# Transposing K in two row halves of the TensorE array, in a cached-attention kernel

## The chip, the cores and the metric

The kernel runs on one core of one Trainium2 chip. The metric is the device time of one execution in microseconds (us), as the median of several runs.

Engine names as the profile has them: PE is the TensorE's matmul side, PEld its weight loads, DVE the VectorE, ACT the ScalarE, SP the engine that issues the loads. "DMA" is what the 16 DMA engines move. The "granted clock" is the share of TensorE's full clock that the profile records as let through; in all traces here it is 1.0 or 0.5, and a figure between them is a mean over time.

## The reference

Attention of 4 new positions in each of 32 batches against a cache of 2,048 keys; 32 query heads share 4 key/value heads; head size 128; all bfloat16. Cut to what matters:

```python
B, Sq, D = 32, 4, 1024
Hq, Hkv, Sk, Dh = 32, 4, 2048, 128
q = (x @ wq).reshape(B, Sq, Hq, Dh).transpose(0, 2, 1, 3)
k = jnp.repeat(k_cache, Hq // Hkv, axis=1)
v = jnp.repeat(v_cache, Hq // Hkv, axis=1)
scores = jnp.einsum("bhqd,bhkd->bhqk", q, k) * Dh ** -0.5
p = softmax(scores)
o = jnp.einsum("bhqk,bhkd->bhqd", p, v)
return o.transpose(0, 2, 1, 3).reshape(B, Sq, Hq * Dh) @ wo
```

K and V are 2 MB each per batch, 128 MB in all; the two weight matrices are 8 MB each.

## The kernel before

It is a hand-scheduled program: each engine has its own list of instructions, with semaphores between them. One batch i is one turn of the loop:

```python
for i in range(B):
    pe_qk(i)                      # 16 matmuls: scores into four PSUM banks (ps_s)
    softmax_max(i)                # DVE
    if i >= 2: pe_ot(i - 2); ot_evac(i - 2)      # (every 8th batch: oproj, 128 matmuls)
    for f in (0, 1): pe_fill(i + 1, f); evac(i + 1, f)
    softmax_exp(i)                # ACT
    for f in range(2, 8): pe_fill(i + 1, f); evac(i + 1, f)
    softmax_rinv(i)
    if i >= 1: pe_pv(i - 1); o_evac(i - 1)       # 64 matmuls on four column tiles
    for f in range(2): pe_pt(i, f); evac_pt(i, f)  # 16 transposes of P
```

K arrives with keys on the partitions; QK needs it with the head size there, so each batch needs 64 transposes of 128x128 (tiles t of K_sb). They come in eight "fills" of 8, each into one PSUM bank of a ring of four, and ACT (fills 0, 1, 4, 6) or DVE (2, 3, 5, 7) copies the bank to KT_sb:

```python
def pe_fill(b, f):
    buf, waits = slot(("kt", b, f))           # next of the four ring banks, once free
    buf = slot_of["kt", b, f] = buf.bitcast(BF16)
    for q in range(TB):                        # TB = 8
        c, v = q // (TB // C), q % (TB // C)
        t = c * TV + f * TB // C + v
        p.op("pe", lambda e, q=q, t=t: e.transpose(
            buf[:, q * 128:(q + 1) * 128], K_sb[:, b % NKB, t, :], ident[:, :]),
            waits + [("k", b), "ident"] if q == 0 else [], ("fill", b, f) if q == TB - 1 else None)
```

Each matmul or transpose becomes two instructions of TensorE, a weight load and a matmul (5,929 of each on the page below). A batch has 2 x (64 + 64 + 16 + 16 + 1) = 322 of them; in the trace it is 323 with a wait, and an output projection adds 256 to every eighth batch.

## Time and profile before

| | before |
|---|---|
| time, median of 3 | 387.33 us (387.23 to 387.41) |
| span of the profiled run | 385.4 us |
| data moved | 152.32 MB, 416 GB/s in the stretch 200 to 300 us |
| mean granted clock of TensorE | 0.946 |
| one batch while data is the limit | 10.0 us |
| one batch while catching up (compute alone) | 8.6 us |

The chain of waits that ended last, by engine, shares of the span:

```profile
DMA 59%; PE 17%; ACT 13%; DVE 7%; issue 2%; SPq 1%
```

Groups of instructions: line, engine, operation, tiles, shapes, count | busy us, mean ns of one | idle time before them and what ended it.

```profile
L207 PE MATMUL ps_r<-ident,K_sb 128*128 128x128 bf16 x2048 | 142.6, 229 | 66.0 <-DMA K_sb<-in_k_cache_dram 40.8
L217 DVE COPY KT_sb<-ps_r 128x1024 bf16<-128x1024 bf16 x128 | 148.0, 1216 | 40.0 <-PE ps_r L207 39.8
...
L248 PE MATMUL ps_r<-V_sb,PT_sb 128*32 128x128 bf16 x2048 | 36.7, 223 | 17.2 <-ACT KT_sb L219 12.8
...
L225 PE MATMUL ps_r<-ident,P_sb 128*128 128x128 bf16 x512 | 35.1, 223 | 1.8 <-ACT P_sb L285 1.4
L240 PE MATMUL ps_s<-KT_sb,QT_sb 128*32 128x512 bf16 x512 | 34.3, 386 | 2.5 <-DVE KT_sb L217 1.7
```

The idle time of L207 ends on the landing of K; PE, DVE and ACT all have slack. The timeline of PE over one batch (start us, duration us, engine, line, what; in brackets the idle time before and what ended it):

```profile
271.34 1.08 PE L248 MATMUL ps_r<-V_sb,PT_sb 128*32 128x128 bf16 x64 [0.92 <-ACT KT_sb L219]
272.35 1.07 PE L225 MATMUL ps_r<-ident,P_sb 128*128 128x128 bf16 x16
273.35 1.05 PE L240 MATMUL ps_s<-KT_sb,QT_sb 128*32 128x512 bf16 x16
...
275.85 2.41 PE L207 MATMUL ps_r<-ident,K_sb 128*128 128x128 bf16 x40 [1.29 <-DMA K_sb<-in_k_cache_dram]
278.50 1.07 PE L207 MATMUL ps_r<-ident,K_sb 128*128 128x128 bf16 x16 [0.24 <-ACT KT_sb L219]
...
281.36 1.08 PE L248 MATMUL ps_r<-V_sb,PT_sb 128*32 128x128 bf16 x64 [0.93 <-ACT KT_sb L219]
```

PV, P transposes, QK, then 1.29 us of waiting for K, then 64 K transposes, then PV again 10.0 us after the last one. Forty transposes take 2.41 us with the last one's latency.

### The profile page before, as it was taken

Reading aid. Unit: us, or ns where it says so; the run is one execution under the profiler, and the core shown is the slowest. Engines: PE = TensorE matmul, PEld = TensorE weight load, DVE = VectorE, ACT = ScalarE, POOL = GpSimd, SP = SyncE. Lnnn points to the kernel's source line nnn. Section 1 sums busy time; section 2 is a strip of 40 time slices with the busy share of each in tenths; the row PEclk is TensorE's granted clock in tenths of the full one; section 3 lists DMA queues with packets and bytes.
Section 4 is the critical chain, followed back from the end, with each engine's and each line's share of the span. In section 5 each row is a group of like instructions: output and inputs, shape, how many; then the busy total and the mean of one; then the engine's idle time right before and its main releaser. Section 6 shows DMA issues by size and latency. Waiting matters only on the chain.

```text
span 385.4 us, 12595 instructions
## 1 busy us (share of the span) xinstructions
PE 280.9 (73%) x5929; PEld 229.5 (60%) x5929; DVE 274.1 (71%) x299; ACT 208.5 (54%) x261; POOL 0.7 (0%) x6
## 2 busy tenths in 40 slices
PE   1876888676383967888767778877767888776756
PEld 1875766465282856666655566665645676565545
DVE  0017999683552984899888859998868859987850
ACT  1005777355161646676666627766646566666620
POOL 0000000000000000000000000000000000000000
PEclk9998999886976899999999999999999999999978
DMA  7999999999999999999999999999999999999930
GB/s 328 432 432 416 418 417 398 413 410 395 413 409 409 419 416 414 419 413 418 417 419 417 417 414 417 416 416 411 417 417 417 418 420 415 417 418 410 375 143 9
DMA packets 27251, 152.32 MB, mean 395 GB/s; under 512 B 1472, under 2 KB 1984, under 8 KB 22592
## 3 DMA queue, kind: packets, MB, share of 16 engines
q1 hardware_dynamic: 27104, 151.49, 96.1%
q8 instruction: 46, 0.75, 0.8%
q10 hardware_dynamic: 96, 0.03, 0.0%
q14 instruction: 5, 0.04, 0.0%
HBM read 151.26 MB, written 0.26 MB: 393 GB/s over the span
## 4 chain that ended last, share of the span: by engine, by line
DMA 59%; PE 17%; ACT 13%; DVE 7%; issue 2%; SPq 1%
DMA K_sb<-in_k_cache_dram 59%; ACT KT_sb L219 7%; ACT P_sb L285 6%; DVE KT_sb L217 4%; PE ps_r L207 4%; PE ps_r L248 3%; PE ps_r L296 3%; PE ps_r L225 3%; PE ps_s L240 3%; DVE mx L280 2%; PE ps_s L296 1%; DVE PT_sb L231 0%; SPq L129 0%; PE ps_r L271 0%; ACT oT_sb L275 0%
## 5 line engine op out<-in xcount | busy, mean ns | idle before, releaser
L207 PE MATMUL ps_r<-ident,K_sb 128*128 128x128 bf16 x2048 | 142.6, 229 | 66.0 <-DMA K_sb<-in_k_cache_dram 40.8
L217 DVE COPY KT_sb<-ps_r 128x1024 bf16<-128x1024 bf16 x128 | 148.0, 1216 | 40.0 <-PE ps_r L207 39.8
L207 PEld LDWEIGHTS ps_r<-ident,K_sb 128*128 128x128 bf16 x2048 | 125.7, 103 | 82.2 <-DMA K_sb<-in_k_cache_dram 41.9
L219 ACT ACTIVATE KT_sb<-ps_r 128x1024 bf16<-128x1024 bf16 x128 | 124.5, 1025 | 72.1 <-PE ps_r L207 72.0
L280 DVE TENSOR_REDUCE mx<-ps_s 128x1 f32<-128x2048 f32 x32 | 73.3, 2292 | 7.1 <-PE ps_s L240 4.6
L285 ACT ACTIVATE P_sb<-ps_s,negmx 128x2048 bf16<-128x2048 f32 x32 | 63.0, 1969 | 2.2 <-DVE negmx L281 2.1
L231 DVE COPY PT_sb<-ps_r 128x1024 bf16<-128x1024 bf16 x64 | 41.4, 686 | 16.7 <-PE ps_r L225 15.2
L248 PE MATMUL ps_r<-V_sb,PT_sb 128*32 128x128 bf16 x2048 | 36.7, 223 | 17.2 <-ACT KT_sb L219 12.8
L248 PEld LDWEIGHTS ps_r<-V_sb,PT_sb 128*32 128x32 bf16 x2048 | 31.0, 98 | 22.7 <-ACT KT_sb L219 19.4
L275 ACT ACTIVATE oT_sb<-ps_r 128x128 bf16<-128x128 bf16 x31 | 8.6, 277 | 55.6 <-PE ps_r L271 55.6
L225 PE MATMUL ps_r<-ident,P_sb 128*128 128x128 bf16 x512 | 35.1, 223 | 1.8 <-ACT P_sb L285 1.4
L240 PE MATMUL ps_s<-KT_sb,QT_sb 128*32 128x512 bf16 x512 | 34.3, 386 | 2.5 <-DVE KT_sb L217 1.7
L225 PEld LDWEIGHTS ps_r<-ident,P_sb 128*128 128x128 bf16 x512 | 29.4, 99 | 5.4 <-ACT P_sb L285 1.6
L240 PEld LDWEIGHTS ps_s<-KT_sb,QT_sb 128*32 128x32 bf16 x512 | 10.8, 96 | 13.3 <-issue 2.8
L187 DVE CAST QT_sb<-ps_r 128x512 bf16<-128x512 f32 x2 | 1.3, 686 | 22.4 <-PE ps_r L176 22.4
L265 ACT ACTIVATE o_sb<-ps_r,rinv 128x128 bf16<-128x128 f32 x31 | 11.4, 367 | 9.8 <-PE ps_r L248 9.8
L189 ACT ACTIVATE QT_sb<-ps_r 128x512 bf16<-128x512 f32 x2 | 1.1, 594 | 26.0 <-PE ps_r L176 26.0
L176 PE MATMUL ps_s<-P_sb,w_sb 128*128 128x128 bf16 x128 | 9.4, 232 | 7.2 <-DMA w_sb<-in_wq_dram 7.2
L296 PE MATMUL ps_r<-w_sb,oT_sb 128*32 128x256 bf16 x384 | 11.5, 273 | 2.6 <-issue 1.4
L176 PEld LDWEIGHTS ps_s<-P_sb,w_sb 128*128 128x128 bf16 x128 | 8.3, 105 | 7.8 <-issue 4.4
L296 PEld LDWEIGHTS ps_r<-w_sb,oT_sb 128*32 128x32 bf16 x384 | 10.0, 97 | 3.7 <-issue 2.5
L271 PEld LDWEIGHTS ps_r<-ident,o_sb 128*128 128x128 bf16 x31 | 3.0, 98 | 12.7 <-issue 12.7
(30 smaller groups left out, 58.9 us busy)
## 6 DMA issues: line engine op xcount, KB each, us to landing
K_sb<-in_k_cache_dram SPq DMA_DIRECT2D x32, 2048.0 KB, 25.4
V_sb<-in_v_cache_dram SPq DMA_DIRECT2D x31, 2048.0 KB, 27.3
w_sb<-in_wq_dram SPq DMA_DIRECT2D x4, 2048.0 KB, 14.8
w_sb<-in_wo_dram SPq DMA_DIRECT2D x4, 2048.0 KB, 24.7
V_sb<-in_v_cache_dram SPq DMA_DIRECT2D x4, 512.0 KB, 15.8
P_sb<-in_x_dram SPq DMA_DIRECT2D x1, 256.0 KB, 2.8
out_dram<-y_sb SPq DMA_DIRECT2D x14, 16.0 KB, 12.1
out_dram<-y_sb ACTq DMA_DIRECT2D x2, 16.0 KB, 1.6
```

The lines of the kernel that those rows point to most:

```text
L176: p.op("pe", lambda e, kt=kt, h=h: e.matmul(ps_q(h), lhsT=w_sb[:, kt, h * Dh:(h + 1) * Dh], rhs=xT_sb[:, kt, :], start=(kt == 0 and h % 4 ...
L207: p.op("pe", lambda e, q=q, t=t: e.transpose(buf[:, q * 128:(q + 1) * 128], K_sb[:, b % NKB, t, :], ident[:, :]), waits + [("k", b), "iden ...
L217: p.op("dve", lambda e: e.tensor_copy(dst, src), waits, ("kt", b, f))
L219: p.op("act", lambda e: e.activation(dst, src, ACT.Copy), waits, ("kt", b, f))
L225: p.op("pe", lambda e, q=q: e.transpose(buf[:, q * 128:(q + 1) * 128], P_sb[:, (8 * f + q) * 128:(8 * f + q + 1) * 128], ident[:, :]), wai ...
L231: p.op("dve", lambda e: e.tensor_copy(PT_sb[:, 8 * f:8 * f + 8, :].rearrange("p t q -> p (t q)"), buf), [("ptf", i, f)] + ([("pv", i - 1)] ...
L240: p.op("pe", lambda e, c=c, g=g: e.matmul(ps_s[32 * g:32 * (g + 1), c * 512:(c + 1) * 512], lhsT=QT_sb[:, i, REP * g:REP * (g + 1), :], rh ...
L248: p.op("pe", lambda e: e.matmul(buf[32 * g:32 * (g + 1), 0:Dh], lhsT=PT_sb[:, t, 32 * g:32 * (g + 1)], rhs=V_sb[:, i % NVB, g, t, :], star ...
L265: p.op("act", lambda e: e.activation(o_sb[:, :], buf[:, 0:Dh], ACT.Copy, scale=rinv[:, i:i + 1]), [("pv", i), ("rinv", i)] + ([("oT", i - ...
L280: p.op("dve", lambda e: e.tensor_reduce(mx[:, i:i + 1], ps_s[:, :], AX.X, ALU.max), [("qk", i)], ("mx", i))
L285: p.op("act", lambda e: e.activation(P_sb[:, :], ps_s[:, :], ACT.Exp, bias=negmx[:, i:i + 1], scale=scale, accum_out=ssum[:, i:i + 1]), [( ...
L296: p.op("pe", lambda e, h=h, j=j: e.matmul(buf[32 * j:32 * (j + 1), 0:NC], lhsT=oT_sb[:, h, 32 * n:32 * (n + 1)], rhs=wo_sb[:, h, NC * j:NC ...
```

## The change

The intent: two half tiles, each on its own 64 rows of the array, should be worked on at once and so take less than one whole tile. The keys of a tile are split into rows 0 to 63 and 64 to 127; each half is transposed by its own 64x128 row tile into its own bank, 64 columns at a time. Fills therefore go in groups of two banks, and KT_sb gets the half as an outer dimension.

```diff
-        KT_sb = sbuf("KT_sb", [128, TV, G, R * C], BF16)
+        KT_sb = sbuf("KT_sb", [128, 2, TV, G // 2, R * C], BF16)
@@ pe_fill
+            if f % 2:
+                return
+            bufs, waits = [], []
+            for h in range(2):
+                buf, w = slot(("kt", b, f + h))
+                buf = slot_of["kt", b, f + h] = buf.bitcast(BF16)
+                bufs.append(buf)
+                waits += w
-            for q in range(TB):
+            for q in range(2 * TB):
 ... (c, v, t of the doubled group)
-                p.op("pe", lambda e, q=q, t=t: e.transpose(
-                    buf[:, q * 128:(q + 1) * 128], K_sb[:, b % NKB, t, :], ident[:, :]),
+                for h in range(2):
+                    p.op("pe", lambda e, q=q, t=t, h=h: e.transpose(
+                        bufs[h][:, q * 64:(q + 1) * 64], K_sb[64 * h:64 * h + 64, b % NKB, t, :],
+                        ident[64 * h:64 * h + 64, 64 * h:64 * h + 64]),
 ... (waits at the first, both "fill" marks at the end of the group)
@@ evac
+            dst = KT_sb[:, f % 2, v0:v0 + 2 * TB // C, :, :].rearrange("p v g (r c) -> p (v g) r c", c=C)
@@ pe_qk
-                        rhs=KT_sb[:, 4 * c:4 * (c + 1), g, :],
+                        rhs=KT_sb[:, g // 2, 4 * c:4 * (c + 1), g % 2, :],
```

## The prediction

> **What bounds the kernel now.** The DMA queue. In the table of stretches its share is 0.99 to 1.03 from 10 us to 360 us; the page counts 152.32 MB, which at the 416 GB/s of 200:300 is 366 us of the 385.4 us span. The chain of waits is 59% "DMA K_sb". One batch (4 MB of K and V) takes 10.0 us: in the timeline the K transposes start at 265.84 and 275.85 us, after 1.3 us of waiting for K both times. The compute chain of a batch is shorter: 8.57 us between 310.21 and 318.78 us, where PE was catching up after an output projection. So some 1.5 us per batch are slack. After the last K lands (358.56 us) comes a tail of 26.9 us which nothing hides.

> **What the change does.** 2,048 K transposes (128x128; 40 in a row start within 2.24 us, 56 ns each) become 4,096 half ones (64 rows, N=64) on alternating row halves, with twice the weight loads, each still 128 columns. The order of the program shows four groups of 32 per batch instead of eight of 8. Each group waits for two PSUM buffers and hands both over at its end. Evictions (ACT 1,025 ns, DVE 1,216 ns), their order and access patterns, QK, PV, softmax and all DMA keep shape and count.

> **Cost of the PE part.** In the trace, 64 PV matmuls on four column tiles take 1.08 us, 17 ns for one load and one matmul; if row halves overlap as well, a pair costs 34 ns (issue) to 56 ns (no gain), so a batch's transposes cost 2.2 to 3.6 us instead of 3.6.[...]

> **How much is critical.** Of the eight fills only the first (0.63 us) is on the batch's chain; the rest hide behind evictions and the exp (2 x 0.97 ACT evictions, 1.95 exp, 0.9 eviction), then PV, PT, QK. The first eviction waited for 8 transposes (0.45 us); it now waits for 16 tiles' worth (0.5 to 0.9 us). The chain moves by 0 to +0.4 us and stays under 10 us: no effect while the DMA is the limit. In the tail that counts once. K buffers come free a little earlier, but loads are already 25 us in flight, so bandwidth isn't touched.

> **Prediction: 387.2 us, 8 in 10 between 384.5 and 391.5; faster by over 2%: 0.03, within 2%: 0.87, slower: 0.10.**

> **What would show it right.** DMA share still about 1.0 at 416 GB/s up to 360 us; batch period 10.0 us; L215 PE busy time falling from 142.6 us to 80 to 130 us; ACT and DVE busy times unchanged; tail from last K landing 26 to 28 us.

> **What would make it wrong.** (1) Row halves that don't overlap[...]: [...]the time goes to 400 us or more, DMA share below 0.95. (2) The granted clock: it fell to 0.50[...] (72 to 80 us, 86 to 94 us). With sparser PE work it may fall in more batches; a cold iteration took 9.1 us (107.1 to 116.2), still under 10, but the tail could move by 1 to 3 us: it ran PT and PV at 0.50 (372 to 377 us), oproj at 1.00. (3) Handover in pairs that stalls ACT and DVE on PSUM buffers; four buffers, two per group, leave just one group ahead.

The cost of the PE part comes to 2.2 to 3.6 us a batch, from the 17 ns and the 56 ns of the trace, and the 387.2 us rest on that and on the data queue. The case against it, risk 1, was summed to 400 us or more. The falls to 0.50 are in the trace.

## More of the kernel before

The page of the kernel before: busy time by engine; then, over 40 equal slices of the span, the granted TensorE clock in tenths, the share in which the DMA engines were busy in tenths, and the rate; then the DMA queue q8, with packets, MB and share.

```profile
PE 280.9 (73%) x5929; PEld 229.5 (60%) x5929; DVE 274.1 (71%) x299; ACT 208.5 (54%) x261; POOL 0.7 (0%) x6
...
PEclk9998999886976899999999999999999999999978
DMA  7999999999999999999999999999999999999930
GB/s 328 432 432 416 418 417 398 413 410 395 413 409 409 419 416 414 419 413 418 417 419 417 417 414 417 416 416 411 417 417 417 418 420 415 417 418 410 375 143 9
...
q8 instruction: 46, 0.75, 0.8%
```

The DMA row is at 9 from the second slice until the tail: the queue of data is the limit. PEclk is at full speed from slice 15 on, until the tail. Queue q8 carries 16,384-byte blocks of instructions.

## The result, and the profile after

The changed kernel took **420.48 us** (419.1 to 420.5, three runs), against 387.33 us before: ratio 1.0844, 95% interval 1.0811 to 1.0878. Ratios here are the mean time of one kernel's fast runs over that of the other's of the same rounds, so not quite the ratio of the medians. The prediction was 387.2 us, range 384.5 to 391.5, and "within 2%" had 0.87.

The page after, the same lines:

```profile
PE 273.6 (66%) x7977; PEld 213.8 (51%) x7977; DVE 275.8 (66%) x299; ACT 209.7 (50%) x261; POOL 0.7 (0%) x6
...
PEclk9995789866586886768695986698886998879989
DMA  8999999999999999999999986999999978998600
GB/s 341 432 426 409 419 414 412 394 409 410 400 418 416 416 415 422 411 419 412 414 393 370 386 369 255 363 394 401 385 380 405 364 300 305 380 421 307 223 9 8
...
q8 instruction: 62, 1.02, 1.0%
```

PE's busy time went down by 7 us, and the time up by 33. Two rows look different: PEclk is below full speed in most slices, and DMA falls below 9 in several slices from the middle of the span on, with 371 GB/s between 200 and 300 us instead of 416. Queue q8 has 62 packets instead of 46. The chain:

```profile
PE 41%; ACT 19%; DMA 19%; DVE 14%; issue 6%; SPq 0%
```

DMA is 19% of it instead of 59%. The groups:

```profile
L228 DVE COPY KT_sb<-ps_r 128x1024 bf16<-128x1024 bf16 x128 | 149.2, 1217 | 20.6 <-PE ps_r L215 20.1
L215 PE MATMUL ps_r<-ident,K_sb 64*128 64x64 bf16 x4096 | 94.4, 203 | 100.2 <-ACT KT_sb L230 43.2
...
L259 PE MATMUL ps_r<-V_sb,PT_sb 128*32 128x128 bf16 x2048 | 55.6, 283 | 11.5 <-issue 6.4
L236 PE MATMUL ps_r<-ident,P_sb 128*128 128x128 bf16 x512 | 49.6, 272 | 10.5 <-issue 6.9
...
L251 PE MATMUL ps_s<-KT_sb,QT_sb 128*32 128x512 bf16 x512 | 42.1, 451 | 3.1 <-issue 1.6
```

L215, the half transposes, is what the change hoped for: 94.4 us busy instead of 142.6: 64 half transposes start within 0.98 us (below, at 280.04; 1.17 us with the end of the last), 31 ns for a pair of halves against 56 ns for a whole tile. The copies of DVE are as before, and so are those of ACT (1,025 ns in both). But instructions that the change did not touch got slower: PV (L259) 55.6 us instead of 36.7, P transposes (L236) 49.6 instead of 35.1, QK (L251) 42.1 instead of 34.3. The timeline of PE, the batch from 269 us and the one from 280 us:

```profile
269.45 1.03 PE L215 MATMUL ps_r<-ident,K_sb 64*128 64x64 bf16 x55
271.55 0.30 PE L215 MATMUL ps_r<-ident,K_sb 64*128 64x64 bf16 x9 [1.07 <-issue]
...
274.98 0.96 PE L259 MATMUL ps_r<-V_sb,PT_sb 128*32 128x128 bf16 x55
277.62 0.34 PE L259 MATMUL ps_r<-V_sb,PT_sb 128*32 128x128 bf16 x9 [1.69 <-issue]
...
280.04 1.17 PE L215 MATMUL ps_r<-ident,K_sb 64*128 64x64 bf16 x64
...
285.56 1.74 PE L259 MATMUL ps_r<-V_sb,PT_sb 128*32 128x128 bf16 x64
287.24 1.89 PE L236 MATMUL ps_r<-ident,P_sb 128*128 128x128 bf16 x16
289.06 1.28 PE L251 MATMUL ps_s<-KT_sb,QT_sb 128*32 128x512 bf16 x16
```

Two different things can be seen here, and each costs its batch more than the 1.5 us that used to be slack.

- **At 271.55 and 277.62 PE stands still with nothing to wait for** ("issue"): 1.07 us within a group of half transposes, and 1.69 us within PV, after 55 of its 64 matmuls. No semaphore stands there.
- **From 285.56 on, PV takes 1.74 us, the P transposes 1.89 us and QK 1.28 us**, where before they took 1.08, 1.07 and 1.05. Between 286 and 288 us the granted clock was 0.50; it had been 1.00 from 270 to 284 us.

From 131 us (where the weights are loaded) to the last QK, the batch took 11.61 us on average, output projections included, instead of 10.22; the mean clock in this time was 0.81 instead of 1.00. 23 batches of 1.39 us more are 32 of the 33 us.

**Where the stalls sit.** The trace holds every instruction of PE and PEld and every DMA packet. I numbered the instructions of TensorE in order of start, and listed queue q8's packets beside them.

```
                                             before    changed
instructions in TensorE's stream             11,905    16,054
16,384-byte packets on q8                        46        62
instructions per packet (stream / packets)      259       259
stalls "issue" over 0.25 us after 50 us whose
  first instruction is number 192..195 mod 256     7        32
  their sum                                   7.9 us   35.2 us
from the end of a q8 packet to the restart                 1.25 to 1.62 us in all 32
median distance of two q8 packets after 131 us  6.5 us    6.3 us
```

In both kernels the distances crowd a little above 6 us: 17 of 45 before and 35 of 61 in the changed kernel lie between 5.9 and 6.6 us. (Seven in the changed kernel are below 5 us; in five of these seven gaps the DMA moved less than 180 GB/s.) So by these counts one packet brings 256 instructions (16,384 / 256 = 64 bytes each), and the stalls sit at one fixed place of every block, 1.25 to 1.62 us after a packet has ended. I read this as TensorE having run out of instructions. The stall at 277.62 us is instruction 10,177 = 39 x 256 + 193, and the last packet had ended 1.46 us earlier. In the kernel before, the seven stalls of this kind came to 7.9 us; in the changed kernel the 32 came to 35.2 us.

This gives a sum. If a block takes 6.2 us, TensorE gets at most 41 instructions a us. A batch of the changed kernel has 453 instructions: 453 / 256 x 6.2 = 11.0 us, and with an eighth of an output projection 11.7 us; 11.6 were measured. A batch before has 323: 7.8 us, or 8.6 with the projections, below the 10.0 us of the data. (When I wrote the expectations below I took 464 and 336, which is 11 and 13 too many, and left the projections out of the sum; the table has the counts of the traces.)

### The profile page after: what moved, and what is told of

Same layout as the page of the kernel before. It is cut to its first block, busy times and chain, and to the rows that moved or that the text cites. A ratio compares the mean times of both kernels' runs of the same rounds, so it can differ in the third digit from the quotient of the medians.

```text
span 417.3 us, 16744 instructions
## 1 busy us (share of the span) xinstructions
PE 273.6 (66%) x7977; PEld 213.8 (51%) x7977; DVE 275.8 (66%) x299; ACT 209.7 (50%) x261; POOL 0.7 (0%) x6
## 4 chain that ended last, share of the span: by engine, by line
PE 41%; ACT 19%; DMA 19%; DVE 14%; issue 6%; SPq 0%
DMA K_sb<-in_k_cache_dram 13%; PE ps_r L259 11%; ACT KT_sb L230 11%; PE ps_r L236 10%; PE ps_s L251 8%; ACT P_sb L296 8%; DVE KT_sb L228 7%; PE ps_r L215 7%; DVE mx L291 6%; DMA w_sb<-in_wq_dram 5%; PE ps_r L307 3%; PE ps_s L307 1%; PE ps_r L282 1%; PE ps_s L176 0%; DVE negmx L292 0%
## 5 line engine op out<-in xcount | busy, mean ns | idle before, releaser
L215 PE MATMUL ps_r<-ident,K_sb 64*128 64x64 bf16 x4096 | 94.4, 203 | 100.2 <-ACT KT_sb L230 43.2
L230 ACT ACTIVATE KT_sb<-ps_r 128x1024 bf16<-128x1024 bf16 x128 | 126.7, 1025 | 54.8 <-PE ps_r L215 54.4
L215 PEld LDWEIGHTS ps_r<-ident,K_sb 64*128 64x128 bf16 x4096 | 79.9, 103 | 114.6 <-ACT KT_sb L230 47.2
L291 DVE TENSOR_REDUCE mx<-ps_s 128x1 f32<-128x2048 f32 x32 | 73.3, 2292 | 18.9 <-PE ps_s L251 18.0
L242 DVE COPY PT_sb<-ps_r 128x1024 bf16<-128x1024 bf16 x64 | 42.8, 689 | 53.4 <-PE ps_r L236 53.3
L259 PE MATMUL ps_r<-V_sb,PT_sb 128*32 128x128 bf16 x2048 | 55.6, 283 | 11.5 <-issue 6.4
L236 PE MATMUL ps_r<-ident,P_sb 128*128 128x128 bf16 x512 | 49.6, 272 | 10.5 <-issue 6.9
L259 PEld LDWEIGHTS ps_r<-V_sb,PT_sb 128*32 128x32 bf16 x2048 | 45.9, 128 | 17.5 <-issue 8.6
L236 PEld LDWEIGHTS ps_r<-ident,P_sb 128*128 128x128 bf16 x512 | 42.3, 125 | 16.6 <-issue 11.6
L251 PE MATMUL ps_s<-KT_sb,QT_sb 128*32 128x512 bf16 x512 | 42.1, 451 | 3.1 <-issue 1.6
L251 PEld LDWEIGHTS ps_s<-KT_sb,QT_sb 128*32 128x32 bf16 x512 | 12.2, 106 | 19.4 <-issue 9.3
L307 PEld LDWEIGHTS ps_r<-w_sb,oT_sb 128*32 128x32 bf16 x384 | 10.1, 97 | 5.6 <-issue 4.5
```

The lines of the kernel that those rows point to most:

```text
L215: p.op("pe", lambda e, q=q, t=t, h=h: e.transpose(bufs[h][:, q * 64:(q + 1) * 64], K_sb[64 * h:64 * h + 64, b % NKB, t, :], ident[64 * h:6 ...
L230: p.op("act", lambda e: e.activation(dst, src, ACT.Copy), waits, ("kt", b, f))
L236: p.op("pe", lambda e, q=q: e.transpose(buf[:, q * 128:(q + 1) * 128], P_sb[:, (8 * f + q) * 128:(8 * f + q + 1) * 128], ident[:, :]), wai ...
L242: p.op("dve", lambda e: e.tensor_copy(PT_sb[:, 8 * f:8 * f + 8, :].rearrange("p t q -> p (t q)"), buf), [("ptf", i, f)] + ([("pv", i - 1)] ...
L251: p.op("pe", lambda e, c=c, g=g: e.matmul(ps_s[32 * g:32 * (g + 1), c * 512:(c + 1) * 512], lhsT=QT_sb[:, i, REP * g:REP * (g + 1), :], rh ...
L259: p.op("pe", lambda e: e.matmul(buf[32 * g:32 * (g + 1), 0:Dh], lhsT=PT_sb[:, t, 32 * g:32 * (g + 1)], rhs=V_sb[:, i % NVB, g, t, :], star ...
```

## The experiments

Three theories:

- **Refill theory**: 40% more instructions a batch exceed the rate at which instruction blocks arrive.
- **Clock theory**: sparser PE work lets the granted clock drop to 0.50, and PV, P transposes and QK, which lie on the batch's chain, take twice as long.
- **Handover theory**: groups of two PSUM banks out of four starve or delay ACT and DVE.

Twelve kernels, with the kernel before run beside them (386.6 to 387.0 us in every group).

| run | what | instructions a batch | time us | ratio to before [95%] | mean clock |
|---|---|---|---|---|---|
| (change) | | 453 | 420.48 | 1.0844 [1.0811, 1.0878] | 0.81 |
| e1 | before + 128 semaphore increments a batch | 451 | 804.40 | 2.0807 [2.0762, 2.0852] | 0.64 |
| e2 | before + 64 of them | 387 | 493.26 | 1.2765 [1.2733, 1.2798] | 0.79 |
| e3 | before, groups of two banks | 325 | 386.38 | 0.9993 [0.9961, 1.0026] | 0.96 |
| e4 | change, half of the tiles | 325 | 402.21 | 1.0381 [1.0345, 1.0417] | 0.78 |
| e5 | before + 66 short matmuls a batch | 455 | 414.21 | 1.0718 [1.0667, 1.0768] | 0.95 |
| e6 | change + dense matmuls | 485 | 430.38 | 1.1121 [1.1060, 1.1183] | 0.92 |
| e7 | e4 + dense matmuls | 357 | 395.72 | 1.0232 [1.0168, 1.0295] | 0.86 |
| e8 | before, most V loads left out | 323 | 347.36 | 0.8977 [0.8958, 0.8996] | 0.98 |
| e9 | change, most V loads left out | 453 | 388.92 | 1.0036 [0.9998, 1.0075] | 0.83 |
| e10 | change in every second batch | 453 and 323 | 407.26 | 1.0524 [1.0501, 1.0547] | 0.85 |
| e11 | before, dummy matmuls in the tail | 323 | 385.12 | 0.9952 [0.9939, 0.9964] | 0.96 |
| e12 | before + 30 short matmuls a batch | 383 | 388.68 | 1.0048 [1.0028, 1.0067] | 0.96 |

(The clock is that of the profiled run; for e6, whose profiled run was slow, the mean of its three fast runs. All ratios are to the kernel before, also those of e8 and e9, whose results are wrong.)

### e1 and e2: idle instructions as filler (failed as a test)

```diff
@@ pe_fill of before, behind the transposes
+            for _ in range(16 if b else 0):          # e2: 8
+                p.op("pe", lambda e: e.sem_inc(filler, 1))
```

> The kernel before, with 16 idle instructions (increments of a semaphore that nobody reads) behind each of the eight K fills of batches 1 to 31: 3,968 more in TensorE's instruction stream, about as many as the change adds (4,096), with no more matmuls, the same PSUM handover and the same matmul density. Refill theory (instruction blocks of 16 KB reach TensorE no faster than one in about 6.2 us while the data queue is full, and 464 instructions a batch need 11.2 us): 405 to 425 us, refills 6.2 us apart, data queue no longer full. Clock theory and handover theory: 386 to 390 us.

> As e1, with 8 instead of 16 behind each fill: 400 instructions a batch. Refill theory: 400/256 x 6.2 = 9.7 us a batch, just under the 10.08 us that the data takes, so 386 to 393 us. If the idle instructions themselves cost sequencer time: about half of the rise of e1.

Both expectations missed widely: 804 and 493 us. The filler is not idle: in the timeline of e1 from 400 to 426 us, mostly 1.4 to 2.0 us (once 0.8) pass with PE idle at each place where 16 increments stand. The blocks on q8 (62) then came 12 us apart in the median, so refills were not the limit. The runs say nothing on the refill theory. They do say that PE's clock falls with idle time even where all matmuls are the long ones of before: in e2 it went to and fro between 0.50 and 1.00 every 6.8 us, with a mean of 0.79.

### e3: the handover alone

```diff
@@ pe_fill of before, in groups of two banks as in the change, full 128-row transposes
+            for q in range(TB):
+                for h in range(2):
+                    t = c * TV + (f + h) * TB // C + v
+                    ... e.transpose(bufs[h][:, q * 128:(q + 1) * 128], K_sb[:, b % NKB, t, :], ident[:, :])
```

> Only the handover of the change: full 128-row transposes as before, but issued alternately into two PSUM banks, both waited for before the first and both handed over after the last. Handover theory: a good part of the 33 us, over 395 us. Refill and clock theories: 386 to 390 us (instruction count and stream as before).

386.38 us, ratio 0.9993: the handover theory falls. Its one effect is on batches that catch up, 8.94 us instead of 8.64, which the data hides. Its mean clock was 0.96.

### e4: the instruction count of before, with even sparser PE work

```diff
@@ pe_fill of the changed kernel
-            for q in range(2 * TB):
+            for n in range(TB):
+                q = n % 4
@@ evac
-            src = buf.rearrange("p (c m r) -> p m r c", c=C, r=R)
+            src = buf[:, 0:256].rearrange("p (m r o) -> p m r o", r=R, o=1).broadcast_to([128, 8, R, C])
```

> Wrong result on purpose. The changed kernel with only 8 of the 16 tiles of each group transposed (in row halves, as in the change; evictions read the same quarter of the bank four times, so their size stays): the instruction count of before, 336 a batch, but TensorE streams even less than in the changed kernel. Clock theory (sparser work lowers the granted clock, and slow PV, PT and QK lengthen the batch): at least 410 us, mean clock under 0.82. Refill theory: 385 to 391 us.

402.21 us at a clock of 0.78, so between the two: the refill theory's "385 to 391" falls, and so does the clock theory's "at least 410". With the instruction count of before, and three stalls at the block's place (3.5 us in all), a loss of 15.6 us remains. (By the edit, the 8 tiles of a group are four tiles, each transposed twice. The copies of ACT and DVE took as long as before, 1,024 and 1,214 ns in the median, so the changed reading pattern is not the cause.) Clock and refills of e4:

```profile
PEclk9996666665675686666868698888888888888888
...
q8 instruction: 46, 0.75, 0.8%
```

The timeline of PE over a part of one batch of e4:

```profile
204.17 0.61 PE L216 MATMUL ps_r<-ident,K_sb 64*128 64x64 bf16 x16 [1.50 <-ACT KT_sb L231]
206.50 0.61 PE L216 MATMUL ps_r<-ident,K_sb 64*128 64x64 bf16 x16 [1.72 <-DVE KT_sb L229]
207.24 1.90 PE L260 MATMUL ps_r<-V_sb,PT_sb 128*32 128x128 bf16 x64
209.07 1.89 PE L237 MATMUL ps_r<-ident,P_sb 128*128 128x128 bf16 x16
```

There is no stall in the middle of a group. PE works 0.6 us out of each 2.3 us while ACT and DVE evict, the clock is at 0.50 from 204.2 to 211.0 us, and PV and the P transposes run at half speed. The batch takes 10.1 to 11.1 us instead of 10.0. The records show the clock at 1.0 or 0.5 only, in phases of 3.4 us or multiples of it (in the kernel before 3.41, 6.83, 10.24, 34.13 us and so on, apart from the cut-off last one). (A side note: the comparison with the reference still passed, although a part of K was replaced by another. With these inputs it seems hardly to see K.)

### e5: the instruction count of the change, with denser PE work

```diff
@@ pe_fill of before
+            extra = 11 if b and f >= 2 else 0
+            for m in range(extra):
+                p.op("pe", lambda e, m=m: e.matmul(
+                    raw[:, 0:64], lhsT=K_sb[:, b % NKB, m, :], rhs=ident[:, 0:64],
+                    start=True, stop=True, skip_group_check=True), ...)
```

> The kernel before, with 11 short matmuls (128 rows, N=64, into the bank that is then overwritten) ahead of each of the fills 2 to 7 of batches 1 to 31: 132 more instructions a batch, 468 instead of 336, about as many as in the changed kernel (464), while TensorE works more densely than before, not less. Refill theory: 468/256 x 6.2 = 11.3 us a batch, so 400 to 425 us, with stalls at rows 193 and 194 of every 256, 1.3 us after a refill ended, and a clock near 1.0. Clock theory alone: 386 to 391 us.

414.21 us, with the clock nearly full:

```profile
PEclk9999999999699999899999998999989999989988
...
q8 instruction: 62, 1.02, 1.0%
```

There were 35 stalls at numbers 192 to 195 of the blocks, 51.2 us in all, and blocks came 6.1 us apart in the median. The timeline of PE, PV and P transposes of two batches:

```profile
201.13 0.95 PE L254 MATMUL ps_r<-V_sb,PT_sb 128*32 128x128 bf16 x53
204.11 0.35 PE L254 MATMUL ps_r<-V_sb,PT_sb 128*32 128x128 bf16 x11 [2.02 <-issue]
...
212.39 1.08 PE L254 MATMUL ps_r<-V_sb,PT_sb 128*32 128x128 bf16 x64
213.40 1.07 PE L231 MATMUL ps_r<-ident,P_sb 128*128 128x128 bf16 x16
```

In the batch at 204 us PV stops for 2.02 us after 53 matmuls; in the next one it runs through, at full speed. Batches without a stall took 8.8 to 9.1 us, so the added matmuls are not themselves the limit. Row halves and low clock are absent here, and 27 of the 33 us are back: **the refill theory is right for most of the loss, and needs nothing of the row split but its instruction count.**

### e6 and e7: the change, and e4, with the stream filled up again

```diff
@@ pe_fill of the change (e6) and of e4 (e7), ahead of each group
+            for n in range(2 if b else 0):
+                for h in range(2):
+                    ... e.matmul(raws[h][:, :], lhsT=K_sb[64 * h:64 * h + 64, b % NKB, 0, :],
+                        rhs=K_sb[64 * h:64 * h + 64, b % NKB, 4 * n:4 * n + 4, :], ...)   # N = 512
```

> The changed kernel, with two N=512 matmuls for each row half ahead of each group (banks that are then overwritten): TensorE streams again about as much as before the change, at 32 instructions more a batch (496). Clock theory alone: mean clock over 0.93 and 386 to 396 us. Refill theory alone: clock irrelevant, 496/256 x 6.2 = 12.0 us a batch, 415 to 440 us. Both at work: 400 to 430 us with a clock over 0.93, because the refills still bind.

> Wrong result on purpose. e4 (which took 402 us at a clock of 0.78 with the instruction count of before) with the same N=512 matmuls as e6: 368 instructions a batch, which refills allow (8.9 us). If the low clock is what made e4 slow: clock over 0.93 and 386 to 390 us. If it was anything else in e4 (row halves, groups): still about 402 us or more.

e6: the fast runs took 429 to 432 us with the clock at 0.91 to 0.92 (the profiled run was slow, 436.5 us, and is left out). A higher clock and more instructions made the changed kernel slower, not faster, as the refill theory asks. In the trace (of the slow run) a batch at full clock and without a stall took 9.1 us, so the added matmuls themselves are not the limit. The clock did not quite reach the 0.93 that was expected.

e7: 392.7 to 397.8 us at 0.85 to 0.87; at 2% the verdict is unclear. The clock came back only in part (0.95 would be full, as before), and of e4's 15.6 us some 8.8 us are left over the kernel before of the same rounds. Neither expected number was met. The trace of e7 shows more than its time, because the clock differs from batch to batch of the same program. From the QK at 247.84 us to the next, the clock was 1.00 and the batch took 8.89 us; from the QK at 277.13 us to the next, it was 0.83 and the batch took 10.20 us. Both wait equally long for the copies (1.36 and 1.05 us) and not for K. PV, and the P transposes in part, ran at half speed in the second:

```profile
254.71 1.09 PE L268 MATMUL ps_r<-V_sb,PT_sb 128*32 128x128 bf16 x64
...
284.24 1.90 PE L268 MATMUL ps_r<-V_sb,PT_sb 128*32 128x128 bf16 x64
286.07 1.33 PE L245 MATMUL ps_r<-ident,P_sb 128*128 128x128 bf16 x16
```

The same instructions with no stall thus take 1.3 us more where the clock falls: **the low clock by itself lengthens a batch, by nearly all of the slack.** The changed kernel shows the other side. Its batch from the QK at 380.49 us to the one at 389.16 us, at a clock of 1.00 and with one short stall that the copies hid, took 8.67 us, as before the change (8.64). Row halves and groups of two banks therefore cost the chain next to nothing when clock and instructions are there.

### e8 and e9: half the data on the queue

```diff
-            load_v(b)
+            if b < NVB:
+                load_v(b)
+            else:
+                ... later batches wait for the last of these V loads, and read the old V
```

> Wrong result on purpose. The kernel before, with V loaded for three batches only (later batches read the old V), so that the data queue has 2 MB a batch instead of 4 and is no longer full. Compute then sets the pace, 8.65 us a batch by the unstalled batches of the profile before: 330 to 345 us. It is the partner of e9.

> Wrong result on purpose. The changed kernel with the same cut of the V loads. If refills are slow because they queue behind data: refills closer than 5 us where they follow each other at once, no stalls at rows 193 and 194, and only the clock's part of the loss left, 9 to 10.4 us a batch, 340 to 380 us. If a refill takes its 6.2 us whatever the data queue does: 464/256 x 6.2 = 11.2 us a batch again, 400 us or more.

e8 took 347.36 us, e9 388.92 us, both slower than expected by 2 and 9 us. What e9 was for is clear, though. Its clock, rate and refills:

```profile
PEclk9997569978796968888888876888888888888888
...
GB/s 328 431 431 416 419 418 401 399 405 405 426 333 220 220 79 172 216 206 204 220 220 220 218 140 109 193 244 218 218 213 204 220 218 162 216 85 2 3 2 8
...
q8 instruction: 62, 1.02, 1.1%
```

In the first 114 us, where the weights still keep the queue full, blocks came 6.0 to 6.6 us apart where they followed each other at once, and seven stalls came in this time and just after it. After that, with the queue at about 220 GB/s, they came as close as 3.4 us, and after 131 us only three stalls (3.3 us) are left. The distance follows the load of the moment, too: in all 16 gaps of under 4.5 us the DMA moved less than 240 GB/s, and in the nine in which it moved over 310 GB/s the distance was 5.3 to 6.9 us. **So a refill is slow here because the data queue is full.** A batch of e9 then took 10.2 us against 8.6 in e8, at a clock of 0.83 against 1.00. That is what the clock costs where no data and next to no refill stands in front of it: some 1.6 us a batch, and 34.5 of the 41.6 us between the two kernels fell in the 23 batches after 121 us, the three stalls included. With the full data the batch takes 10.0 us anyway, which would explain why e4 shows only 15.6 us of it.

### e10: every second batch

```diff
+        def halves(b):
+            return b % 2 == 0
@@ pe_fill, evac, pe_qk
+            if not halves(b):  ... as before the change
```

> The change in every second batch (even ones row halves in groups of two banks, odd ones as before): 400 instructions a batch on average. Refill theory alone: 9.8 us a batch, under the 10.08 us of the data, so 386 to 390 us and few stalls. If the loss simply goes with the number of row-half batches: about 403 us. With both theories at work, refills no longer binding and the clock low in half of the batches: 388 to 398 us.

407.26 us, outside what either theory alone or both were expected to give; 25 stalls at the block's fixed place, 32.3 us. My expectation took the average of the two kinds of batch for what counts. The likely reason for the miss, worked out after the run, is that a batch of 453 instructions cannot draw on the quiet of its neighbour, whose own compute takes 8.6 us. Taking both, (11.0 + 8.6) / 2 = 9.8 us, plus the three output projections of 6.2 us spread over 23 batches, 0.8 us, is 10.6 us a batch; measured were 11.1. The remaining 0.5 us (the clock was 0.87) was not taken apart, and no run tests this sum.

### e12: 383 instructions in every batch

The edit, shown against e5:

```diff
-            extra = 11 if b and f >= 2 else 0
+            extra = 5 if b and f >= 2 else 0
```

> e5 (414 us) with 5 instead of 11 short matmuls ahead of each of the fills 2 to 7: 396 instructions in every batch, where e10 had 464 and 336 in turn. If refills are a rate limit (one block of 256 in 6.2 us, so up to 416 instructions in the 10.08 us of a batch): 386 to 391 us. If each added instruction costs in proportion, as e10 suggested: 387 + 27 x 5/11 = 399 us.

388.68 us, ratio 1.0048. The page has the data queue full to the end:

```profile
DMA  8999999999999999999999999999999999999940
...
q8 instruction: 53, 0.87, 0.9%
```

Seven more blocks than before cost 1.6 us, nine more again (e5) cost 26 us. e12 has 17 stalls (18.9 us) too, but nearly all of this fits into the slack of its batches. So there is a threshold, not a price for each instruction. The two runs place it between 383 and 455, and the sum puts it at the lower end: 256 / 6.2 x 10.08 = 416 instructions in the time of a batch's data, less 32 for its eighth of an output projection, is 384.

### e11: a warm tail, a try at beating both

In the tail, before's own PE idled and ran its last P transposes and PV at a clock of 0.50:

```profile
371.85 1.89 PE L225 MATMUL ps_r<-ident,P_sb 128*128 128x128 bf16 x16 [1.43 <-ACT P_sb L285]
...
374.53 3.16 PE L248 MATMUL ps_r<-V_sb,PT_sb 128*32 128x128 bf16 x64 [0.68 <-DVE PT_sb L231]
```

```diff
+        def warm(buf, n, waits):
+            for m in range(n):
+                ... e.matmul(buf[:, :], lhsT=ident[:, :], rhs=KT_sb[:, 0:4, 0, :], ...)   # N = 512
@@ pe_pv: 5 of them if i == B - 2;  pe_pt: 6 of them if i == B - 1 and f == 0
```

> A try at beating both: the kernel before, with 11 dummy N=512 matmuls in the 2.9 us in which TensorE idles in the tail (5 ahead of PV of batch 30, 6 ahead of the P transposes of batch 31), so that the clock does not fall to 0.50 where PT took 1.89 us and PV 3.16 us. If the clock stays at 1.0 these take 1.07 and about 1.1 us: 2.9 us less, about 384 us. If the dummies only delay the P transposes: 387 us or a little more.

385.12 us, ratio 0.9952 [0.9939, 0.9964]: 0.5% faster than before (by the 2% rule "same", but clear of noise), and so the fastest of all here that is correct. The tail now:

```profile
371.82 1.07 PE L233 MATMUL ps_r<-ident,P_sb 128*128 128x128 bf16 x16
...
373.82 1.76 PE L256 MATMUL ps_r<-V_sb,PT_sb 128*32 128x128 bf16 x64 [0.88 <-DVE PT_sb L239]
```

The clock was 1.00 in every 2 us stretch from 364 to 382 us. The P transposes gained the 0.8 us that was expected, PV (for all its 64) 1.40 us instead of 2.1. The gain was 1.8 us of the expected 2.9.

## Why the prediction was wrong

**What failed first is a missing term.** The section on cost knew two prices of a half transpose, its issue and its stream, and from 34 to 56 ns a pair concluded 2.2 to 3.6 us a batch. This is right, and even a little high: 31 ns, 2.0 us. It had no term for bringing the instructions to the engine. The section before it states "4,096 half ones ... with twice the weight loads", which is 128 more instructions a batch on 322; the page's q8 line had 46 packets of 16 KB; the trace had them as close as 5.9 us, most of the close ones a little above 6. From these three, some 11 us a batch could have been worked out before the run, on the guess that packets can come no closer. e5 shows this term alone: +27 us. e12 shows that it is a threshold, and e9 that the delay comes from the full data queue (6.0 to 6.6 us a block behind it, as little as 3.4 us at about 220 GB/s).

**The second step that failed is a size.** "a cold iteration took 9.1 us (107.1 to 116.2), still under 10". The clock was named under "what would make it wrong (2)", but its size was taken from a batch that only began cold; PE worked there through its 64 transposes without a pause, and the clock was back at 1.00 by 112 us, before PV began at 113.05. With sparse transposes it is the other way round: the clock falls during the transposes and is low in steps that are on the chain (e4: 0.50 from 204.2 to 211.0 us, with PV at 1.90 and the P transposes at 1.89 us). e4 measured 10.1 to 11.1 us a batch, e9 10.2 us, and e7 10.20 us in a batch with the low clock against 8.89 us in one without.

**"The chain moves by 0 to +0.4 us and stays under 10 us: no effect while the DMA is the limit"** therefore failed twice over, since either of the two alone eats the 1.5 us of slack. They don't add up: alone they cost 27 us (e5) and 15.6 us (e4), together 33. How much of the 33 is whose is not a question with one answer; by e5 and e4, which stand in for the changed kernel, some 27 would remain without the clock's fall and some 16 without the slow refills, and both have to go for the time of before.

What held: the row halves overlap (31 ns a pair; risk 1 did not come); L215's busy time of 94.4 us lies in the 80 to 130 us predicted; ACT's and DVE's copies are unchanged; the handover in pairs (risk 3) cost nothing that showed in the time (e3). What did not: DMA share of 1.0 at 416 GB/s up to 360 us (371 GB/s between 200 and 300 us), and the batch period of 10.0 us (11.6 with the output projections, where it was 10.2 before).

The overlap of loads with matmuls does not by itself explain the gain. In the changed kernel the loads and matmuls of the two row halves overlap: one load and one matmul start every 15 to 16 ns. But in the kernel before, 40 whole-tile transposes, all on the same 128 rows, also started within 2.19 us at a clock of 1.00, 56 ns apart, though a load lasts 98 ns in the profile, and each load starts within 12 ns after the start of the matmul before it. So loads overlapped before as well. Why a pair of halves takes 31 ns where a whole tile takes 56 was not shown.

**What stays open.** What exactly lowers the clock: the share of time in which PE works, or how many columns it streams. Full-length matmuls with idle time lowered it (e2, 0.79), short ones without idle time did not (e5, 0.95), so idle time is enough; e7, which restored the stream with few long matmuls, got only to 0.86. Nor is it clear how much idling it takes: in the kernel before, the clock fell 2.0, 3.0, 4.6 and 2.1 us after the end of PE's last work (at 73.96, 87.62, 104.68 and 118.33 us), and in e4 it fell at 204.2 us after a pause of 1.5 us. Open too are e10's last 0.5 us a batch. Also, no run separates the two causes in the changed kernel itself behind a full data queue; e4 and e5 stand in for it.
